# Longer load rows, more output buffers, later stores and single last stores in a fused attention and token-mixing kernel

## The chip, the cores and the metric

The kernel runs on one core of a Trainium2 chip. The metric is the time of one execution on the device in microseconds (us), lower is better. The kernel before takes 130.08 us (median of 3 runs, 130.0 to 131.48). Each run is fast or slow (slow: over 1.5% above the fastest of the same kernel).

The engines are named as in the profile: PE (TensorE) with PEld, its weight loads; DVE (VectorE), ACT (ScalarE), POOL (GpSimd) and SP (SyncE), which issues nearly all DMAs. An eviction is the copy that moves a finished tile from `ps`, which PE writes, to a buffer, for the output to `o_sb` (a median 0.585 us on ACT for a tile of 128x512 in the trace of before).

## The reference

Attention without softmax, in linear form, feeds a token-mixing layer. Cut to what matters:

```python
def _attn_ref(q, k, v):                       # (8, 8, 576, 64) each
    q_p, k_p = phi(q, cos_w, sin_w), phi(k, cos_w, sin_w)   # relu, times cos and sin of position
    kv = np.einsum('bhsf,bhsd->bhfd', k_p, v)
    z = np.sum(k_p, axis=2)
    num = np.einsum('bhsf,bhfd->bhsd', q_p, kv)
    den = np.einsum('bhsf,bhf->bhs', q_p, z)[..., None] + 1e-06
    return num / den

def _moe_ref(x, w_q, w_k, w_out):             # x: (8, 576, 512)
    W_tok = scale * np.einsum('bsd,btd->bst', x @ w_q, x @ w_k)
    mixed = np.einsum('bst,btd->bsd', W_tok, x)
    return np.maximum(mixed, 0.0) @ w_out
```

The inputs q, k and v are 28.3 MB in float32, the output is 9.44 MB.

## The kernel before

A "pair" here is two pairs of heads, that is four of the eight heads of a batch; there are 16, two to a batch. A "block" of the output, numbered 0 to 3, is two batches, 9 tiles of 128 rows, stored in groups of two, two, one, two and two tiles. (The blocks of 256 PE instructions in the experiments are something else.) Every engine's instructions are put in order by a list scheduler in the kernel (`plan_order`) that runs when the kernel is built. Each engine, and SP's queue of DMAs, then goes through its own list in the order of the list. So an instruction whose data isn't there holds up what stands behind it in that list: in the changed kernel two tiles evicted by 109.0 us were stored from 124.0 us on, behind stores of tiles that were evicted later.

```python
PAIRS = ((0, 1), (2, 3), (4,), (5, 6), (7, 8))     # tiles of one store group
CS = ((0, 5), (5, C9))                             # columns: 1280 and 1024 bytes of a row

def load(H, parts=((0, C9),), names=("q", "k", "v"), engs=()):
    for nm in names:
        raw[nm, H] = inp.tile([P, 2, HC], FP32, name="raw")      # 6 buffers
    for lo, hi in parts:
        for nm in names:
            eng = nc.scalar if lo == 0 and nm in engs else nc.sync
            eng.dma_start(raw[nm, H][:, :, lo * D:hi * D],
                          srcs[nm][b][:, h0:h0 + 2, lo * D:hi * D])

def store(bp, g, qs):                              # two DMAs of 64 partitions
    n = len(PAIRS[g])
    for hi in range(2):
        qs[hi].dma_start(..., o_sbs[bp, g][64 * hi:64 * hi + 64, 0:n, :])
...
                elif e == "DMA":
                    key = t            # plan_order: DMAs in the order in which they can start
...
        if kind == "load":
            load(j, parts=CS, names=(b,))
        elif kind == "st":
            last = b == B // 2 - 1 and j >= 2
            store(b, j, (nc.sync, A if last else nc.sync))
```

## Time and profile before

| | before |
|---|---|
| time, median | 130.08 us |
| span of the profiled execution | 129.5 us |
| busy share: PE, DVE, ACT, POOL | 79%, 73%, 61%, 55% |
| last load issued | 95.9 us |
| k multiply of pair 15 begins | 101.48 us |
| last output tile evicted | 123.75 us |

The strip of the profile cuts the span in 40 slices and gives each engine's busy share in tenths. The k multiply (line 392) comes once a pair and serves as a clock of how far the compute has come. The last eviction splits the end into the compute and what the stores need after it. The lines are in the prediction.

The chain of waits that ended last, as shares of the span:

```profile
PE 47%; DMA 19%; DVE 16%; issue 7%; ACT 3%; POOL 2%; SPq 1%; POOLq 0%
```

### The profile page before, as it was taken

To read this page: it belongs to the slowest core of one execution; us is meant where nothing else is said; L and a number is where in the kernel's file an instruction comes from. 1 tells how busy PE (TensorE), PEld (TensorE's weight loads), DVE (VectorE), ACT (ScalarE), POOL (GpSimd) and SP (SyncE) were. 2 spreads that over 40 slices of the span, in tenths; PEclk is the share of its full clock that TensorE was granted. 3 is DMA by queue.
4 is the path that set the end of the run, shared out by engine and by line. 5 is a ranking of instruction groups with operands and counts; after the bars stand their busy time and mean duration, and the time that the engine had idled before them with its cause. 6 is when DMAs were issued, how large, how long until landed. Compare 5 with 4: busy or idle time off the path is not lost.

```text
span 129.5 us, 5391 instructions
## 1 busy us (share of the span) xinstructions
PE 102.7 (79%) x2262; PEld 63.3 (49%) x2286; DVE 95.0 (73%) x156; ACT 79.6 (61%) x155; POOL 71.1 (55%) x113
## 2 busy tenths in 40 slices
PE   5957694757498998979997878998886999998900
PEld 2334353545375644646664645555564655543400
DVE  1067878999789999899989596999899688314000
ACT  6959435083705677687688755864766376656710
POOL 7720557568489999897289287876652710000000
PEclk9999999999756999999999999999999999999995
DMA  3999999999999999999999999999999754667893
GB/s 86 369 359 357 359 309 354 340 337 383 365 356 358 356 358 366 376 378 369 340 356 360 332 308 379 351 347 323 316 318 326 266 133 123 164 166 189 202 210 128
DMA packets 32968, 39.41 MB, mean 304 GB/s; under 512 B 3248, under 2 KB 27824, under 8 KB 32944
## 3 DMA queue, kind: packets, MB, share of 16 engines
q1 hardware_dynamic: 32304, 38.09, 90.9%
q10 hardware_dynamic: 640, 0.98, 2.6%
q8 instruction: 18, 0.29, 0.9%
q14 instruction: 6, 0.05, 0.1%
HBM read 29.62 MB, written 9.44 MB: 302 GB/s over the span
## 4 chain that ended last, share of the span: by engine, by line
PE 47%; DMA 19%; DVE 16%; issue 7%; ACT 3%; POOL 2%; SPq 1%; POOLq 0%
PE ps L563 20%; DMA raw<-in_k_dram 8%; PE ps L493 6%; DMA raw<-in_v_dram 6%; PE ps L453 4%; DVE qpt_buf L420 4%; PE ps L428 4%; DVE x_sb L466 4%; DMA raw<-in_q_dram 4%; DVE kp L392 3%; PE ps L478 3%; PE ps L523 3%; PE ps L539 2%; PE ps L414 2%; POOL rq_buf L379 2%
## 5 line engine op out<-in xcount | busy, mean ns | idle before, releaser
L563 PE MATMUL ps<-wo_sb,mix_sb 128*128 128x512 bf16 x126 | 34.4, 380 | 2.8 <-DVE xT_buf L368 0.9
L379 POOL TENSOR_SCALAR rq_buf<-raw 128x640 bf16<-128x640 f32 (+1 forms) x30 | 26.2, 887 | 16.9 <-DMA raw<-in_q_dram 13.5
L366 ACT COPY o_sb<-ps 128x512 f32<-128x512 f32 x36 | 21.1, 586 | 12.4 <-PE ps L563 11.0
L392 DVE TENSOR_TENSOR kp<-rk,cossin 128x2304 bf16<-128x2304 bf16 (+2 forms) x17 | 23.0, 1352 | 7.8 <-ACT rk L377 6.1
L466 DVE TENSOR_TENSOR x_sb<-ps,rec 128x640 bf16<-128x640 f32 x32 | 26.4, 825 | 1.1
L404 POOL TENSOR_SCALAR v_buf<-raw 128x640 bf16<-128x640 f32 (+1 forms) x26 | 22.5, 879 | 6.2 <-DMA raw<-in_v_dram 3.0
L420 DVE TENSOR_TENSOR qpt_buf<-ps,cst 128x1152 bf16<-128x1152 bf16 x32 | 22.7, 750 | 1.7 <-PE ps L414 1.7
L379 POOL TENSOR_SCALAR rk<-raw 128x640 bf16<-128x640 f32 (+1 forms) x28 | 18.3, 668 | 8.8 <-DMA raw<-in_k_dram 6.2
L563 PEld LDWEIGHTS <-mix_sb 128*128 128x128 bf16 x144 | 12.2, 97 | 14.5 <-issue 2.4
L428 PE MATMUL ps<-v_buf,kp 64*128 64x65 bf16 x576 | 13.1, 193 | 5.7 <-ACT v_buf L402 2.2
L428 PEld LDWEIGHTS <-kp 64*128 64x128 bf16 x576 | 11.1, 95 | 9.5 <-DVE kp L392 5.0
L453 PE MATMUL ps<-kv_sh,qpt_buf 64*128 64x65 bf16 x320 | 14.5, 193 | 1.2 <-issue 1.2
L551 ACT ACTIVATE mix_sb<-ps 128x576 bf16<-128x576 f32 x24 | 14.5, 655 | 1.4 <-PE ps L539 1.3
L453 PEld LDWEIGHTS <-qpt_buf 64*128 64x128 bf16 x640 | 12.9, 96 | 4.9 <-issue 3.9
L453 PE MATMUL ps<-kv_sb,qpt_buf 64*128 64x65 bf16 x320 | 14.5, 194 | 0.1
L368 DVE COPY xT_buf<-ps 128x640 bf16<-128x640 bf16 (+1 forms) x19 | 8.4, 456 | 6.1 <-PE ps L478 3.9
L289 PE MATMUL ps<-warm 128*128 128x512 bf16 x32 | 11.2, 487 | 1.8 <-DVE warm L285 1.5
L414 PE MATMUL ps<-ident,rq_buf 64*128 64x64 bf16 x288 | 8.3, 193 | 3.3 <-POOL rq_buf L379 1.8
L366 ACT CAST wT_buf<-ps 128x576 bf16<-128x576 f32 x8 | 5.1, 637 | 8.2 <-PE ps L493 8.2
L493 PE MATMUL ps<-xT_buf,wqk_sb 128*128 128x288 bf16 x64 | 10.1, 306 | 0.0
L366 ACT CAST kv_sb<-ps 128x260 bf16<-128x260 f32 x15 | 5.6, 375 | 6.9 <-PE ps L428 5.7
L478 PE MATMUL ps<-ident,x_sb 64*128 64x64 bf16 x288 | 7.6, 190 | 2.3 <-DVE x_sb L466 1.5
(51 smaller groups left out, 123.1 us busy)
## 6 DMA issues: line engine op xcount, KB each, us to landing
out_dram<-o_sb SPq DMA_DIRECT2D x30, 256.0 KB, 5.2
raw<-in_q_dram SPq DMA_DIRECT2D x16, 320.0 KB, 6.0
raw<-in_v_dram SPq DMA_DIRECT2D x16, 320.0 KB, 6.2
raw<-in_k_dram SPq DMA_DIRECT2D x15, 320.0 KB, 5.8
raw<-in_q_dram SPq DMA_DIRECT2D x16, 256.0 KB, 5.9
raw<-in_k_dram SPq DMA_DIRECT2D x16, 256.0 KB, 6.0
raw<-in_v_dram SPq DMA_DIRECT2D x16, 256.0 KB, 6.3
wo_f<-in_moe_w_out_dram SPq DMA_DIRECT2D x1, 1024.0 KB, 8.1
```

The source lines that it names most:

```text
L366: nc.scalar.copy(dst, src)
L379: eng.tensor_scalar(dst, src, FMAX, 0.0, op0=ALU.min, op1=ALU.max)
L392: nc.vector.tensor_mul(kp[H][:, 2 * lo:2 * hi], rks[H][:, lo:hi].rearrange("p c i d -> p (c i) d").unsqueeze(2) .to_broadcast([P, 2 * (hi ...
L404: eng.tensor_scalar(dst, src, 1.0, 1.0, op0=ALU.mult, op1=ALU.mult)
L420: nc.vector.tensor_mul(qpt_bufs[H % 2][:, r, :, D:SLOTS * D], bank_h(m)[:, 0:1, 0:HC].to_broadcast([P, 2, HC]), cst)
L428: nc.tensor.matmul(bank(m + r)[:, 0, i * (D + 1):(i + 1) * (D + 1)], kp[H][half_rows(r), 2 * c + i, :, :], v_bufs[H % 3][half_rows(r), c, ...
L453: nc.tensor.matmul(nb[t][:, u, :], qpt_bufs[H % 2][rows, r, w, u * P:(u + 1) * P], mv, start=(u == 0 and w == 0), stop=False)
L466: nc.vector.tensor_tensor(xv[:, h, r], nv[:, :, :, 0:D], rec.to_broadcast([P, 2, SC, D]), op=ALU.mult)
L478: nc.tensor.transpose(bank_h(m + r)[:, 0, k0 * D:(k0 + 1) * D], xs[b][half_rows(r), u, 2 * hp:2 * hp + 2, :], ident[half_rows(r), half_row ...
L493: nc.tensor.matmul(bank(m + nh)[:, 0, 0:hs], wqk_sb[:, dmc, :, :], xT_bufs[b % 2][:, dmc, nh * hs:(nh + 1) * hs], start=(dmc == 0), stop=( ...
L551: nc.scalar.activation(dst, src, AF.Relu, scale=scale_moe)
L563: nc.tensor.matmul(bank(m)[:, 0, :], mixs[bp][:, dmc, rt * P:(rt + 1) * P], wo_sb[:, dmc, :], start=(dmc == 0), stop=(dmc == NDM - 1))
```

## The change

The intent: fetch with longer rows and so less overhead (2304 bytes of a row go as two packets of a median 55 and 46 ns in the trace of before); let loads overtake stores, since the compute waits for loads (POOL for 8.3 us from 80 to 103 us in the trace of before) and no engine that computes waits for a store there; have enough output buffers that nothing waits for a delayed store; and make the last store small. The scheduler's weights were searched anew, and one copy may now go to ACT. The diff, cut to its core:

```diff
-PLAN = dict(mk=1.3, pa=7.848, pc=8.447, pm=8.738, pw=6.677, ... nraw=6, nout=5, ...)
+PLAN = dict(mk=1.3, pa=5.707, pc=6.272, pm=6.005, pw=4.458, ... nraw=6, nout=12, ... ds=11)
...
-        op(("wqc", b), {"DVE": .36}, [("we", b)], 1)
+        op(("wqc", b), {"ACT": .57, "DVE": .36}, [("we", b)], 1)
...
                 elif e == "DMA":
-                    key = t
+                    key = t + (par["ds"] if n[0] == "st" else 0)
...
-    def store(bp, g, qs):
+    def store(bp, g, qs, lo=0, hi=2):          # lo, hi: which tiles of the group
...
         if kind == "load":
-            load(j, parts=CS, names=(b,))
+            load(j, names=(b,))
...
             wout_evac(b, j, m, engs[eng])
+            if b == B // 2 - 1 and j > 4:
+                lo = (j - 5) % 2
+                store(b, (j + 1) // 2, (nc.sync, A), lo, lo + 1)
         elif kind == "st":
-            last = b == B // 2 - 1 and j >= 2
-            store(b, j, (nc.sync, A if last else nc.sync))
+            if b < B // 2 - 1 or j < 3:
+                store(b, j, (nc.sync, nc.sync))
```

More of the change, by code (lines that the diff above doesn't have):

```diff
@@ L22 @@
 EPS_HI = 9.9837780e-07
-PLAN = dict(mk=1.3, pa=7.848, pc=8.447, pm=8.738, pw=6.677, pb=0.821, flex=0.189, poe=11.845,
-            pme=34.049, pmk=1108.864, wo_at=4, nraw=6, nout=5, sw=0, amp=0, seed=99119,
-            sl=0.1, bd=0.2, pact=1)
+PLAN = dict(mk=1.3, pa=5.707, pc=6.272, pm=6.005, pw=4.458, pb=0.728, flex=0.103, poe=2.701,
+            pme=3.798, pmk=160091.523, wo_at=4, nraw=6, nout=12, sw=0, amp=0,
+            seed=32087, sl=0.1, bd=0.2, pact=1, ds=11)
 PAIRS = ((0, 1), (2, 3), (4,), (5, 6), (7, 8))
@@ L500, in wqk_evac, with wq_copy @@
              bank(m, 2)[:, :, 0:hs])
-    def wq_copy(b):
+    def wq_copy(b, eng):
         wq2 = moe.tile([P, S], BF16, name="wq2")
-        nc.vector.tensor_copy(wq2[64:128], wT_bufs[b % 2][0:64, D:SLOTS * D])
+        copy(eng, wq2[64:128], wT_bufs[b % 2][0:64, D:SLOTS * D])
         wqTs[b] = wq2
@@ L571, in wout_evac @@
         copy(eng, o_sbs[bp, g][:, rt - PAIRS[g][0], :], bank(m)[:, 0, :])
-    def store(bp, g, qs):
-        n = len(PAIRS[g])
-        for hi in range(2):
-            qs[hi].dma_start(
-                dataclasses.replace(out, offset=out.offset + out_dest(bp, PAIRS[g][0], hi),
-                                    ap=[[C9 * DM, 64], [2 * DM, n], [1, DM]]),
-                o_sbs[bp, g][64 * hi:64 * hi + 64, 0:n, :])
+    def store(bp, g, qs, lo=0, hi=2):
+        rts = PAIRS[g][lo:hi]
+        for half in range(2):
+            rows = slice(64 * half, 64 * half + 64)
+            qs[half].dma_start(
+                dataclasses.replace(out, offset=out.offset + out_dest(bp, rts[0], half),
+                                    ap=[[C9 * DM, 64], [2 * DM, len(rts)], [1, DM]]),
+                o_sbs[bp, g][rows, lo:lo + len(rts), :])
     A, V, G = nc.scalar, nc.vector, nc.gpsimd
@@ L624, in emit @@
         elif kind == "wqc":
-            wq_copy(b)
+            wq_copy(b, engs[eng])
         elif kind == "wk":
```

## The prediction

The forecast's sum came to 117 + 7.1 = 124.1, and with 0.6 to 124.7. The packet times come from the trace of before.

> **What bounds the kernel now.** I read the strip of 40 slices first, for which resource fills which stretch of the 129.5 us (3.24 us a slice).
>
> ```profile
> span 129.5 us, 5391 instructions
> ...
> PE   5957694757498998979997878998886999998900
> DVE  1067878999789999899989596999899688314000
> ...
> DMA  3999999999999999999999999999999754667893
> GB/s 86 369 359 357 359 309 354 340 337 383 365 356 358 356 358 366 376 378 369 340 356 360 332 308 379 351 347 323 316 318 326 266 133 123 164 166 189 202 210 128
> DMA packets 32968, 39.41 MB, mean 304 GB/s; under 512 B 3248, under 2 KB 27824, under 8 KB 32944
> ```
>
> The DMA row is at 9 from the second slice to the 31st: up to about 100 us the transfers never rest. VectorE is at 9 nearly as long, from 40 to 100 us. Only after that does PE fill its row while DMA and VectorE fall off. So there are two phases: loads until 103 us, and a tail of output matmuls and stores.
>
> Next, the pace of the pairs of heads. The multiplication of k (line 392) runs once a pair on VectorE as soon as k is there, so its starts are a clock. From VectorE's timeline, times in us and durations next:
>
> ```profile
> 13.55 1.35 DVE L392 TENSOR_TENSOR kp<-rk,cossin 128x2304 bf16<-128x2304 bf16 x1
> ...
> 42.97 1.73 DVE L392 TENSOR_TENSOR kp<-rk,cossin 128x2304 bf16<-128x2304 bf16 x1
> ...
> 101.48 1.36 DVE L392 TENSOR_TENSOR kp<-rk,cossin 128x2304 bf16<-128x2304 bf16 x1 [1.17 <-POOL rk L379]
> ```
>
> These are pairs 1, 6 and 15: (42.97 - 13.55)/5 = 5.88 us a pair, then (101.48 - 42.97)/9 = 6.50. A pair loads 3 x 576 KiB = 1.77 MB, 4.97 us at 356 GB/s; pairs 1 to 6 share the queue with 1.31 MB of weights (3.7 us, 0.74 a pair), which makes 5.7. From 47 us stores join: 0.59 MB a pair, and 2.36 MB at 356 GB/s is 6.6 us. Both paces are the DMA's. The windows say the same for the other engines (the columns are the stretch, its length, then busy us of PE, PEld, DVE, ACT, POOL, the clock, DMA share, GB/s):
>
> ```profile
> 50.00:60.00 10.00, 9.03 (x246) 5.94 (x247) 9.48 (x18) 7.78 (x16) 8.64 (x11) 1.00 1.06 374
> ...
> 90.00:100.00 10.00, 8.43 (x230) 5.33 (x232) 9.41 (x17) 6.98 (x16) 5.22 (x9) 1.00 0.99 318
> ...
> 110.00:120.00 10.00, 9.59 (x77) 4.55 (x78) 3.23 (x6) 6.35 (x12) 0.00 (x0) 1.00 0.71 173
> ```
>
> VectorE has half a microsecond in ten left. The DMA is the first bound, and VectorE stands right behind it. GpSimd's waits between 80 and 103 us show who waits for the loads there (us in total, times, longest):
>
> ```profile
> POOL rk L379 <- DMA raw<-in_k_dram: 3.3, 3, 1.7
> POOL rq_buf L379 <- DMA raw<-in_q_dram: 3.2, 3, 1.6
> ...
> POOL v_buf L404 <- DMA raw<-in_v_dram: 1.8, 3, 1.2
> ```
>
> Last, the chain of waits at the end:
>
> ```profile
> 118.66 4.49 PE ps L563 x20
> ...
> 123.17 0.58 ACT o_sb L366
> ```
>
> Five output tiles in 4.49 us, the last eviction done at 123.75, and 5.75 us more for the last stores and the close.
>
> [...] by its packet records a 1024-byte packet takes a median 46 ns, one of 1280 bytes 55 and one of 2048 bytes 84, a slope of about 0.036 ns a byte with 8 to 10 ns on top. [...] Every store here is of 64 partitions; when stores run alone, after 120 us, a 2048-byte packet has a median near 155 ns against 84 before and the rate is 202 to 225 GB/s at a DMA share of 0.85 to 0.9. [...]
>
> **The change part by part.**
> Longer rows. A load has 256 rows, 16 to a DMA engine. Now: 16 x (55 + 46) ns, and two completion packets of 9 ns, 1634 ns; three are 4.90 us, which is the 4.97 found above. After: a 2304-byte packet lies on the line at 91 to 94 ns, so 16 x 92.5 + 9 = 1489 ns. That is 0.145 us a load, and for the 45 loads of pairs 1 to 15, 6.5 us of DMA time. It also halves 90 load issues of some 0.45 us on SyncE, which lie beside transfers and are worth nothing. The price: GpSimd, which still converts in two parts, can't start on the first 5/9 of a tensor, under 0.7 us, felt once or twice.
>
> Deferred stores, twelve buffers. Before the last load is issued (95.9 us) nine store groups have gone: four pairs and a single of the first block, three pairs and a single of the second, 9 x 0.524 MB less two halves = 4.19 MB, 11.8 us at 356 GB/s. The planner's key puts a store behind loads whose buffer comes free up to 11 us later, that is, a shift of nearly two pairs. The groups issued at 82.1, 87.4 and 91.7 should fall behind the last load: a single and two pairs, 1.31 MB, 3.7 us. There are five groups to a block, so twelve buffers hold over two of the four blocks, so no output matmul should wait for one.
>
> So the DMA could bring the last load some 10 us sooner (6.5 + 3.7). I don't credit all of it, because VectorE's work has to be done too. From its groups, work that can't leave it: k multiply 23.0, rotation of q 22.7, normalisation 26.4 + 6.8, sum 78.9 us, 4.93 a pair. The rest of its 95.0, about 16 us or 1.0 a pair, can go to ScalarE (61% busy), and the 4.2 us of the copy at line 504 become movable by this change. If half the 16 moves, VectorE needs 5.4 a pair, at 95% use 5.7; PE's back-to-back runs in the trace (for a pair 0.68 kv, 0.75 numerators, 0.8 transposes; for a batch 2.4 of mixing; for two batches 9 tiles of 0.97) also come to 2.2 + 1.2 + 2.2 = 5.6. Call the pace 5.85: pair 15's multiply at 13.3 + 14 x 5.85 = 95, against 101.5. That is the gain I take, 6.5 us.
>
> From there to the last eviction are 22.3 us now, filled by output matmuls. I leave it at 22, so the last eviction is at 117.
>
> Single stores. The last store moves 128 KB a half rather than 256: at some 220 GB/s 0.6 us less a half, and two queues issue it; 5.75 becomes about 4.3. But there is a danger in the order. The single stores are written right behind their evictions, whereas the groups of tiles 0 to 4 carry the 11 us penalty, also when no load is left to give way to. Tile 8 follows tile 0 by less than 11 us (in the trace of before their evictions start at 123.17 and 112.81), so groups 0 to 2 of the last block, and perhaps the two groups ahead of them, stand on SyncE's queue behind single stores that wait for the last evictions. That would leave 1.3 to 2.4 MB to store at 220 to 260 GB/s after 116 us, 5 to 10 us, an end 9 to 11 us behind the last eviction. I give it an even chance: 0.5 x 4.3 + 0.5 x 10 = 7.1. Sum: 117 + 7.1 = 124.1, and 0.6 for the difference of 130.08 and the span: 124.7.
>
> **Rivals.**
> VectorE takes the DMA's place at once, at 6.1 a pair. For it: it is at 9.5 of 10 already. Against: its row dips between 70 and 80 us (7.46) and after 98, and a third of a batch's evictions may move. Then pair 15 comes at 98.7, the end is 127 to 131, "same".
> The deferred stores pile up at the end, as worked out above: if the compute gains only 5 us, the end is 128 to 129 and the change does nothing.
> Everything goes well: pace 5.6, tail 21, stores 4.3: 13.3 + 78.4 + 21 + 4.3 + 0.6, about 118. For it: GpSimd's 8.3 us of load waits after 80 us go. Against: PE would have to run at its back-to-back rate.
> A load ordered ahead of a ready store waits on its buffer and stops SyncE's queue. It costs only if the output buffers run out, and twelve make that unlikely.
>
> **Range and chances.** 118 and 131 are the ends of the rivals; the middle ones lie at 121 to 129. The limit of 2% is 127.5. It takes one of the two bad rivals nearly in full to miss it, and both together to be slower.
>
> **What would show it.** Right: no 1280-byte packets but pair 0's, a 2304-byte packet at 91 to 94 ns, 375 to 395 GB/s in stretches of loads alone; the last load issued before 90 us; pair 15's multiply at 91 to 99; VectorE at 95% or more from 30 us on with fewer evictions. The danger is real if SyncE's last stores are of tiles 0 to 4 and issue after the last eviction, with the end over 8 us behind it. I am wrong if 2304-byte packets take over 100 ns, if pair 15 isn't before 99, or if PE idles for output buffers.

## The result, and the profile after

The changed kernel takes 138.8 us (138.6 to 139.22, 3 runs). The ratio to the kernel before is 1.064, 95% interval 1.052 to 1.076: slower. A ratio here is the mean time of one kernel's fast runs over that of the other's fast runs of the same rounds, so it isn't quite the ratio of the medians quoted.

First the changed kernel's strip (columns are slices of 3.4 us):

```profile
span 137.0 us, 5308 instructions
...
PE   5968747665899797978898987998989999980000
...
DMA  3999999999999999999999999981074400029994
GB/s 105 372 387 391 362 360 391 390 383 391 392 385 393 387 383 346 387 393 402 398 403 403 395 408 401 385 261 48 7 155 91 145 0 0 5 77 240 248 288 142
```

The loads did what was hoped: mostly 383 to 408 GB/s where mostly 340 to 380 stood before, and they are over at about 89 us. The compute did not follow. PE is still full until 122 us, and while it is, the DMA row goes to 0. Then come 12 us in which no engine computes and the DMA is full again.

The clock of the pairs, from the changed kernel's VectorE timeline (start, duration):

```profile
13.39 1.35 DVE L392 TENSOR_TENSOR kp<-rk,cossin 128x2304 bf16<-128x2304 bf16 x1
...
43.20 1.35 DVE L392 TENSOR_TENSOR kp<-rk,cossin 128x2304 bf16<-128x2304 bf16 x1
...
100.43 1.35 DVE L392 TENSOR_TENSOR kp<-rk,cossin 128x2304 bf16<-128x2304 bf16 x1
```

Pairs 6 to 15 take (100.43 - 43.20)/9 = 6.36 us each, against 6.50 before. Pair 15 is 1.05 us earlier, not 6.5.

The end, from the windows of the changed kernel (stretch, length, busy us of PE, PEld, DVE, ACT, POOL, then clock, DMA share, GB/s), and SP's waits from 82 us on (us in total, times, longest):

```profile
110.00:120.00 10.00, 10.00 (x86) 4.55 (x86) 4.06 (x7) 7.62 (x14) 0.00 (x0) 1.00 0.01 2
...
124.60:137.00 12.40, 0.00 (x0) 0.00 (x0) 0.00 (x0) 0.00 (x0) 0.00 (x0) 0.55 0.82 232
```
```profile
SPq L577 <- ACT o_sb L366: 26.4, 5, 14.4
```

For ten microseconds in which finished tiles lie in their buffers, the DMA moves 2 GB/s, because SP waits up to 14.4 us at a stretch for an eviction. After the last eviction (124.57 us) 12.4 us of stores are left, at 232 GB/s: 2.9 MB.

Split at the last eviction, the two profiled spans compare like this: the compute ends at 124.57 against 123.75 (+0.8), the stores need 12.4 against 5.75 (+6.7). Together that is +7.5 us, 137.0 against 129.5. So there are two questions: why the tail is so long, and why the compute got nothing from loads that were over 12 us sooner (89.5 us against 101.8).

### The profile page after: what moved, and what is told of

The parts are those of the page before. It is cut to its first block, busy times and chain, and to the rows that moved or that the text cites. A ratio compares the mean times of both kernels' runs of the same rounds, so it can differ in the third digit from the quotient of the medians.

```text
span 137.0 us, 5308 instructions
## 1 busy us (share of the span) xinstructions
PE 104.0 (76%) x2279; PEld 62.0 (45%) x2279; DVE 90.7 (66%) x144; ACT 86.9 (63%) x168; POOL 66.3 (48%) x111
## 4 chain that ended last, share of the span: by engine, by line
PE 48%; DVE 15%; DMA 10%; issue 7%; ACT 6%; POOL 2%; ACTq 1%; SPq 1%; DVEq 0%; POOLq 0%
PE ps L563 22%; DMA raw<-in_k_dram 6%; PE ps L493 6%; PE ps L453 5%; PE ps L428 5%; DVE x_sb L466 4%; DMA raw<-in_q_dram 4%; PE ps L478 3%; DVE kp L392 3%; PE ps L523 3%; PE ps L539 2%; DVE qpt_buf L420 2%; DVE mix_sb L553 2%; ACT o_sb L366 2%; PE ps L414 2%
## 5 line engine op out<-in xcount | busy, mean ns | idle before, releaser
L563 PE MATMUL ps<-wo_sb,mix_sb 128*128 128x512 bf16 x144 | 37.1, 388 | 1.6 <-issue 0.9
L366 ACT COPY o_sb<-ps 128x512 f32<-128x512 f32 x35 | 20.6, 590 | 13.2 <-PE ps L563 11.7
L379 POOL TENSOR_SCALAR rk<-raw 128x640 bf16<-128x640 f32 (+1 forms) x28 | 19.3, 708 | 16.2 <-DMA raw<-in_k_dram 9.9
L379 POOL TENSOR_SCALAR rq_buf<-raw 128x640 bf16<-128x640 f32 (+1 forms) x28 | 22.8, 830 | 6.9 <-DMA raw<-in_q_dram 6.2
L404 POOL TENSOR_SCALAR v_buf<-raw 128x640 bf16<-128x640 f32 (+1 forms) x26 | 20.2, 795 | 2.3 <-DMA raw<-in_v_dram 1.6
L366 ACT COPY xT_buf<-ps 128x512 bf16<-128x512 bf16 (+1 forms) x25 | 15.1, 638 | 2.0 <-PE ps L478 1.9
L428 PEld LDWEIGHTS <-kp 64*128 64x128 bf16 x576 | 10.6, 94 | 10.0 <-DVE kp L392 5.7
L551 ACT ACTIVATE mix_sb<-ps 128x576 bf16<-128x576 f32 x20 | 12.5, 661 | 1.9 <-PE ps L539 1.7
L553 DVE TENSOR_SCALAR mix_sb<-ps 128x576 bf16<-128x576 f32 x12 | 8.9, 752 | 6.0 <-PE ps L539 6.0
L289 PE MATMUL ps<-warm 128*128 128x512 bf16 x31 | 9.8, 473 | 1.5 <-DVE warm L285 1.5
```

What stands on the lines that cost most here:

```text
L366: nc.scalar.copy(dst, src)
L379: eng.tensor_scalar(dst, src, FMAX, 0.0, op0=ALU.min, op1=ALU.max)
L404: eng.tensor_scalar(dst, src, 1.0, 1.0, op0=ALU.mult, op1=ALU.mult)
L428: nc.tensor.matmul(bank(m + r)[:, 0, i * (D + 1):(i + 1) * (D + 1)], kp[H][half_rows(r), 2 * c + i, :, :], v_bufs[H % 3][half_rows(r), c, ...
L551: nc.scalar.activation(dst, src, AF.Relu, scale=scale_moe)
L563: nc.tensor.matmul(bank(m)[:, 0, :], mixs[bp][:, dmc, rt * P:(rt + 1) * P], wo_sb[:, dmc, :], start=(dmc == 0), stop=(dmc == NDM - 1))
```

## The experiments

Two kernels are compared by their ratios to the kernel before.

The theories. A: the order on SP's queue makes the long tail. C: transfers set the pace before (the prediction). D: PE or VectorE sets it, whatever the loads do. D gave way to F: the load traffic itself slows PE, by delaying the packets that bring PE's instructions (my reading of the packets that the profile calls "instruction"; they start 3.51 us after a block's start with loads in flight and 1.09 without, see section 3).

### 1. a_tail_order: the late stores in their turn

```diff
+    order = plan_order(NB)
+    # every "st" after the last load moves right behind the last eviction it needs
     for n, eng, m in order:
         emit(n, eng, m)
```

> The changed kernel with the order of every engine kept; only the store groups that are written after the last load are put on SyncE's queue right behind the last eviction that they need, so none stands behind a single store of a later tile. Theory A (the queue order made the long tail): the last eviction stays at 124 to 125 us, the stores end some 5 us behind it, span 129 to 130, about 7 us below the 137.0 of the changed kernel. Rival B (the stores of the last blocks need that time whatever their order[...]): span 135 or more.

Measured: 130.55 us, ratio 1.003 (0.999 to 1.007). Last eviction 123.69, span 128.3: the stores end 4.6 us behind it. The window that moved 2 GB/s now reads:

```profile
110.00:120.00 10.00, 9.84 (x65) 4.44 (x66) 3.68 (x7) 7.41 (x14) 0.00 (x0) 1.00 0.65 160
```

Theory A is shown. With no other instruction moved, some 8 us are gone. The changed kernel's stores on SP stood like this, by the order of its instruction list and the issue times in the trace:

```
SP issue at us   what
105.4            second half of tile 4 of block 2
120.9 122.2 123.4   first halves of the single stores of tiles 5, 6, 7 of block 3
124.0 124.6      tiles 5,6 of block 2      (both evicted by 109.0)
125.4            first half of the single store of tile 8 of block 3
126.1 - 132.9    tiles 7,8 of block 2; tiles 0,1 / 2,3 / 4 of block 3
```

The 11 us of the new key hold also when no load is left to give way to, while a single store is written at its eviction. So 2.36 MB of finished output stood behind stores of tiles that didn't exist yet.

### 2. b_long_rows: the long rows alone

```diff
-            load(j, parts=CS, names=(b,))
+            load(j, names=(b,))
```
(in the kernel before)

> The kernel before with one DMA of 2304-byte rows per load and nothing else changed. Theory C (my prediction: transfers set the pace of the pairs in the kernel before): packets of 91 to 96 ns, some 6 us of DMA time less, pair 15's multiply of k at 95 to 97 us instead of 101.5, time 124 to 126. Rival D (PE, working through its planned order, or VectorE sets the pace, and the DMA is kept busy only because loads run ahead into free buffers): pair 15 not before 100, time 128.5 to 130.

Measured: 134.09 us over four runs, of which the two fast are 131.97 and 133.57; ratio 1.019 (1.011 to 1.028), slower. Pair 15 at 102.35 us, later than before, though a 2304-byte packet has a median of 93 ns as predicted and the last load is issued at 90.1 us instead of 95.9. Theory C falls: faster transfers do not help this kernel and cost it something. Two things in its trace speak to why. Against b_two_pairs (section 3, where block starts are explained) its weight loads are 7.6 us late by the end, and around block starts it loses 8.2 us, more than all of it. And SP's queue stands still more often (waits of this kernel, us in total, times, longest):

```profile
SPq L576 <- ACT o_sb L366: 12.3, 7, 3.7
SPq L576 <- ACT kv_sb L366: 11.2, 4, 4.9
...
SPq L576 <- ACT xT_buf L366: 5.8, 3, 2.2
```

Line 576 is the store. These three lines make 29.3 us of waiting for ACT (which of ACT's instructions is named is inferred). All waits of SP at that line for ACT come to 39.5 us here and to 19.3 us before. Part of it lies in the tail; before that, loads behind such a store wait with it. How much of the loss this makes was not tested.

### 3. b_two_pairs and a_two_pairs: no loads from pair 2 on

```diff
-            raw[nm, H] = inp.tile([P, 2, HC], FP32, name="raw")
+            raw[nm, H] = raw[nm, H % 2] if H > 1 else inp.tile([P, 2, HC], FP32, name="raw")
-        for lo, hi in parts:
+        for lo, hi in parts if H < 2 else ():
```

Their outputs are wrong, which doesn't matter for the times.

> Wrong result on purpose: the kernel before, but only pairs 0 and 1 and the weights are loaded; later pairs read those buffers again. It shows the compute of the old order with no load to wait for. Theory C: the pace of pairs 6 to 15 falls from 6.5 to 5.7 us or less, time below 120. Rival D: the pace stays above 6.1, time 124 to 129.

Measured: 125.41 us, ratio 0.964 (0.958 to 0.970). Pairs 6 to 15 at 6.08 us each (40.40 to 95.13), last eviction at 117.28. C missed both of its numbers. D's time came true, and its pace all but (6.08 against "above 6.1"). Yet the loads do cost 5 us of time, against D's idea that they don't matter.

> Wrong result on purpose: the same two-pair loads in the changed kernel, whose tail still has the stores in their late order. Rival D: pair 15's multiply of k stays within 2 us of 100.4 and the time within 2 us of 138.8, since loads are no longer waited for there. Theory C (the changed kernel still waits for loads somewhere): 3 us or more faster.

Measured: 131.63 us, ratio 1.011, with the bad tail still in it (span 129.9, last eviction 117.75, 12.2 behind it). Pair 15 comes at 93.63, 6.8 us sooner than in the changed kernel, and pairs 6 to 15 take 5.75 us each. The expectation of D misses here, and C's number (3 us or more faster) came true with 7.2. But C's reason did not. Loads cost the changed kernel's compute 6.8 us, although after 45 us hardly anything waits for one to land: POOL's waits for loads are 2.4 us in all from 45 to 90 us. Nor do the instructions themselves get slower: in that stretch both traces have a median of 190 ns for the matmuls of line 428 and of 825 ns for VectorE's line 466.

Where does it go? The PE instructions of the changed kernel and a_two_pairs are the same in the same order, so I compared when each weight load starts in the two traces. The delay doesn't grow evenly. It jumps at every 128th weight load, that is, at every 256th PE instruction, since weight loads and matmuls alternate. Of the 6.8 us, 5.6 come within 17 weight loads around such a place; windows of the same width elsewhere in the 128 gather 0.2 us in the median. The share isn't fixed: in a_tail_order, which has the same compute, it is 3.4 of 6.0 us. The profile has a queue that it calls "instruction"; in this run it moved 18 packets of 16384 bytes:

```profile
q8 instruction: 18, 0.29, 0.9%
```

4558 PE instructions (2279 weight loads, 2279 matmuls) are 17.8 blocks of 256, so about one packet to a block. Such a jump in the changed kernel's timeline of weight loads (start, duration; in brackets the idle time before, "issue" where the engine waited for nothing that the profile shows):

```profile
54.42 0.20 PEld L478 LDWEIGHTS <-x_sb 64*128 64x128 bf16 x9 [1.11 <-issue]
...
60.44 0.17 PEld L478 LDWEIGHTS <-x_sb 64*128 64x128 bf16 x7 [0.57 <-issue]
...
66.64 0.10 PEld L428 LDWEIGHTS <-kp 64*128 64x128 bf16 x2 [0.74 <-issue]
...
73.11 0.37 PEld L428 LDWEIGHTS <-kp 64*128 64x128 bf16 x20 [0.29 <-issue]
...
79.31 0.43 PEld L428 LDWEIGHTS <-kp 64*128 64x128 bf16 x24 [0.79 <-issue]
```

Line 478, 428 or whichever it is: the spot is set by the count, not by the operation. They are 6.0 to 6.5 us apart. Put beside the packet records:

```
blocks of 256 PE instructions that begin between 40 and 86 us, worked out from the traces

kernel           blocks   mean length   packet's start after   next block begins within
                          us            block's start, mean    1.7 us of its landing
after              8        6.02            3.51                  8 of 8
before             8        5.69            2.55                  3 of 8
a_two_pairs        9        5.42            1.09                  1 of 9
b_two_pairs        9        5.57            0.83                  0 of 9
```

In the changed kernel every next block begins 1.4 to 1.7 us after a packet landed. I read this as PE waiting for its own instructions; no record says what a packet holds. The packet itself takes about 1.05 us in both cases; it starts 2.4 us later with loads in flight.

### 4. a_unread_loads: the loads run, but nobody reads them

```diff
+            if H < 2:   # keep pairs 0 and 1
+                raw[nm, H] = consts.tile([P, 2, HC], FP32, name=f"keep_{nm}{H}")
+                into = raw[nm, H]
+            else:       # compute on a kept pair, load into a buffer that is never read
+                raw[nm, H] = raw[nm, H % 2]
+                into = inp.tile([P, 2, HC], FP32, name="raw")
```
(in a_tail_order, with nine output buffers; wrong result)

> Wrong result on purpose: the changed kernel with the mended tail; every load is issued as there (one DMA, rows of 2304 bytes), but from pair 2 on the loads go to buffers that nobody reads, and the compute reads pairs 0 and 1 again. Nothing in the compute can wait for these loads to land. Nine output buffers, so that it fits. Theory F (loads hold PE up through its instruction packets): while loads run, PE's blocks of 256 instructions take 6 us and over, the packet coming 3.5 us after the block's start and the next block 1.4 us after the packet; the time is within 2.5 us of a_tail_order's (ratio to the kernel before 0.98 to 1.0). Rival J (what the loads cost is waiting for them to land and for buffers): blocks as in a_two_pairs, 5.4 us, and a ratio of 0.95 or less.

Measured: 131.93 us, ratio 1.008 (0.999 to 1.017), as slow as a_tail_order, which has 1.003. From 42 us to 92 us the blocks take 5.9 to 6.5 us, the packet starts 3.56 us after a block's start in the mean, and 7 of 8 blocks begin within 1.7 us of its landing. The same window in the changed kernel, in this one, and in a_two_pairs (count of weight loads in the second bracket):

```profile
45.00:90.00 45.00, 39.01 (x919) 23.77 (x918) 36.83 (x57) 32.17 (x68) 35.34 (x49) 1.00 1.04 391
```
```profile
45.00:90.00 45.00, 39.22 (x909) 23.70 (x910) 34.76 (x54) 30.73 (x66) 27.00 (x41) 0.96 1.03 388
```
```profile
45.00:90.00 45.00, 42.11 (x1071) 27.41 (x1079) 40.26 (x62) 36.94 (x81) 30.61 (x44) 1.00 0.45 106
```

918 and 910 weight loads with the traffic, 1079 without. The clock of 0.96 in the middle line is a stretch of 3.4 us at half clock, which can cost 1.7 us at most; the missing 169 weight loads stand for some 7 us (an estimate from 45 us for 1079). No wait of the compute for a load from pair 2 on is left that could explain it, so rival J falls. That the traffic slows the compute is shown. That it does so at the block starts is read from the traces; no run could change the packets themselves.

### 5. Smaller loads: a_tail_half_dma, a_tail_short_rows, b_half_dma

```diff
-                eng.dma_start(raw[nm, H][:, :, lo * D:hi * D], srcs[nm][b][:, h0:h0 + 2, lo * D:hi * D])
+                for i0, i1 in ((0, 1), (1, 2)) if H else ((0, 2),):      # two of the four heads at a time
+                    eng.dma_start(raw[nm, H][:, i0:i1, lo * D:hi * D],
+                                  srcs[nm][b][:, h0 + i0:h0 + i1, lo * D:hi * D])
```

("By head" in the expectations means by pair of heads: two heads to a DMA instead of four.) That the packet waits for whole loads ahead of it, and longer for more rows, is theory F's assumption here. The traces had shown the later start alone: 3.51 us with loads, 1.09 without.

> The changed kernel with the mended tail (as a_tail_order), and each load of 576 KB cut in two DMAs by head: still rows of 2304 bytes, but 8 rows instead of 16 for each DMA engine in one DMA. Theory F (between 45 and 90 us PE is held up once in every 256 of its instructions, because the 16 KB packet that brings its next instructions has to wait for whole loads ahead of it on the same DMA engines, and the wait grows with the rows of one DMA): the packet comes 2 us or less after PE enters a block instead of 3.7, blocks of 256 instructions fall from 6.1 to about 5.5 us, time 126 to 128.5. Rival G (the wait is set by the bytes queued, not by the size of one DMA): the packet still comes 3.5 us after, time 129.5 to 131. Rival H (PE's blocks take that long for another reason): no change either, but blocks don't start at a fixed distance behind the packet.

Measured: 129.6 us over five runs, fast ones 128.32 to 129.84, ratio 0.982 (0.971 to 0.993).

> The changed kernel with the mended tail, but loads in two DMAs by columns, with rows of 1280 and 1024 bytes, as in the kernel before. Theory F: packets of instructions wait some 2 us, as in a_tail_half_dma, and the time is 126.5 to 129, though each load takes 0.15 us of DMA time more. Rival G: as a_tail_order or slower, 130 to 132. If short rows were what kept the kernel before at its pace (my prediction), 132 or more.

(Edit: `load(j, parts=CS, names=(b,))` in a_tail_order.) Measured: 131.64 us, ratio 1.002 (0.992 to 1.011). The packet comes 2.93 us after a block's start, the blocks take 5.73. Less waiting than with whole loads (3.25 in a_tail_order), but the time isn't better: F's number missed. The rows of the kernel before, by themselves, are neither its trouble nor a help here.

> The kernel before with rows of 2304 bytes, each load cut in two DMAs by head. Theory F: the loss of b_long_rows (134.1 median, fast runs 132 to 133.6) goes, time 128.5 to 130.5. Rival G: stays at 132 to 134.

Measured: 130.71 us, fast runs 130.07, 130.16 and 131.26, ratio 0.994 (0.982 to 1.005). What the long rows cost the kernel before in whole loads (1.019) is gone; the packet comes 2.45 us after a block's start against 3.14 in b_long_rows.

These three came from a chip on which the kernel before took 132 us, so the size of the effect was repeated in section 8.

### 6. Who issues the single stores: a_tail_sp_only, a_half_pool_store

```diff
-                store(b, (j + 1) // 2, (nc.sync, A), lo, lo + 1)
+                store(b, (j + 1) // 2, (nc.sync, nc.sync), lo, lo + 1)     # a_tail_sp_only
+                store(b, (j + 1) // 2, (nc.sync, G), lo, lo + 1)           # a_half_pool_store
```

> The changed kernel with the mended tail, both halves of the four single stores issued by SyncE. Theory I (each of ACT's own store issues, 0.5 us, stands between two evictions of the last tiles, which therefore follow at 1.2 us instead of 0.86): the last evictions follow at 0.86 us again, the last one ends 1 us sooner, and the time is 0.5 to 1 us below a_tail_order. Rival: SyncE issues one store after the other at 0.6 us and becomes the end, time equal or longer.

In the changed kernel ACT evicts the last tiles and issues their stores in between, 0.49 to 0.54 us an issue:

```profile
120.34 0.59 ACT L366 COPY o_sb<-ps 128x512 f32<-128x512 f32 x1 [0.28 <-PE ps L563]
120.95 0.54 ACTq L577 DMA_DIRECT2D out_dram<-o_sb  x1
121.59 0.59 ACT L366 COPY o_sb<-ps 128x512 f32<-128x512 f32 x1 [0.67 <-PE ps L563]
122.21 0.50 ACTq L577 DMA_DIRECT2D out_dram<-o_sb  x1
122.83 0.59 ACT L366 COPY o_sb<-ps 128x512 f32<-128x512 f32 x1 [0.65 <-ACT o_sb L366]
```

Tiles follow at 1.25 and 1.24 us. In a_tail_sp_only, from the same view:

```profile
120.52 0.59 ACT L366 COPY o_sb<-ps 128x512 f32<-128x512 f32 x1 [0.28 <-PE ps L563]
121.38 0.59 ACT L366 COPY o_sb<-ps 128x512 f32<-128x512 f32 x1 [0.28 <-PE ps L563]
```

They follow at 0.86 us, so the evictions behave as theory I says, and the last ones no longer wait for ACT. The last one still ends at 123.69, as in a_tail_order, because pair 15 was 1.0 us later in this trace. But the time is 132.51 us, ratio 1.007 (0.996 to 1.018), no better than a_tail_order. SP now issues ten stores after 120 us, one every 0.6, the last at 127.1 us, 3.4 us behind the last eviction. The rival came true: the cost moved from ACT's list to SP's.

> a_tail_half_dma with the second halves of the four single stores issued by GpSimd, which is idle by then, instead of ACT. Theory I: the last evictions follow at 0.86 us instead of 1.2, the last ends 1.1 us sooner, and unlike a_tail_sp_only SyncE has no more to issue than before: ratio some 0.008 below a_tail_half_dma, 0.965 to 0.98. Rival: [...] 0.98 to 0.99.

Measured: 130.07 us, ratio 0.991 (0.982 to 1.000). The last evictions follow at 0.86 us and the last ends at 120.96, but the span is 127.0, 6.0 us behind it. The ratio lies just above the rival's range (0.98 to 0.99), not in theory I's. The rival's reason is cut, since no trace had shown it; in this trace the stores on POOL's queue land a median 3.5 us after their issue, against 3.3 on ACT's queue in a_tail_order.

### 7. Two that led nowhere: a_half_depth5, a_all_ready

a_half_depth5 is a_tail_half_dma with `bufs=5` for the loads and each load moved behind the conversion that frees its buffer.

> a_tail_half_dma with five load buffers instead of six, each load moved in SyncE's order behind the conversion that frees its buffer; all other orders kept. With one load fewer queued, theory F expects the instruction packet some 0.3 to 0.7 us earlier and a time equal to a_tail_half_dma or 1 us less (ratio 0.965 to 0.985). If the compute needs the sixth buffer, GpSimd and ScalarE wait for loads and it is slower (0.99 or more).

Measured: 130.88 us, ratio 0.999 (0.990 to 1.008), the packet 2.86 us after a block's start. POOL waits 7.4 us for loads between 40 and 95 us. Nothing is gained by a shorter queue of loads.

a_all_ready moves every store right behind its eviction, also those before the last load (the edit of a_tail_order without its condition).

> The changed kernel with all stores, not only those after the last load, put right behind the eviction that they wait for: no store is behind a later load any more; twelve buffers, long rows, the plan and the single stores stay. If putting stores behind loads matters to the compute, the last load is issued at 88 to 94 us instead of 82 and the time is 2 us or more above a_tail_order (ratio 1.015 or more). Theory F expects the same time within 1 us (0.995 to 1.01), since loads aren't waited for after 45 us, and no less traffic stands ahead of the instruction packets.

Measured: 133.89 us, but three of four runs were slow, the profiled one too, and no ratio came out. The one fast run is 131.5. The last load is issued at 94.4 us in the (slow) profile. Whether the deferral before the last load is worth anything stays open.

### 8. The sizes again, on one chip with five rounds

> The same kernel as a_tail_order, as the base on this chip: ratio 0.998 to 1.008.

> The same kernel as a_tail_half_dma. If the size of one DMA sets how long PE's instructions wait: 1 to 2 us below tail_again (ratio 0.98 to 0.992), with the packet 2.0 to 2.8 us after the start of a block between 45 and 85 us instead of 3.5. If the first result was chance: within 0.5 us of tail_again.

> The same kernel as a_half_pool_store: the last evictions 0.86 us apart, the last one 1 us sooner than in half_again; if that reaches the end, 0.5 to 1 us below half_again, else equal, because SyncE's queue of stores is then what ends last.

> half_pool_again with the second halves of all the last block's stores on GpSimd, so SyncE has three fewer to issue and nothing of ACT's time is used. If SyncE's issuing ends the kernel, 0.7 to 1.5 us below half_pool_again, ratio 0.97 to 0.985; if the rate of the stores ends it, equal.

half_pool_all is half_pool_again with the second halves of all of block 3's stores on POOL's queue (`(nc.sync, G if b == B // 2 - 1 else nc.sync)`).

| kernel | median us | fast runs | ratio to before | 95% interval | packet after block's start, us |
|---|---|---|---|---|---|
| tail_again | 130.55 | 5 | 0.993 | 0.989 to 0.998 | 3.63 |
| half_again | 129.78 | 5 | 0.987 | 0.982 to 0.991 | 2.80 |
| half_pool_again | 129.78 | 4 | 0.986 | 0.981 to 0.991 | (profile slow) |
| half_pool_all | 130.31 | 3 | 0.984 | 0.978 to 0.990 | (profile slow) |

Halving the DMAs brings the packet 0.8 us sooner, the blocks from 6.08 to 5.68 us, and the time some 0.8 us down (0.0065 x 130). One trace each stands behind the packets: the kernel of tail_again had 3.25 us as a_tail_order, so part of the 0.8 can be chance. The direction agrees with theory F in all three places where loads were cut by pair of heads; cut by columns (a_tail_short_rows) they gained no time. The size is less than expected, and the two intervals overlap. Rival G, that the bytes queued alone set the wait, would give no difference, since the bytes are the same; it is made unlikely, not ruled out. Who issues the last block's stores makes no difference that five rounds can show. The best of these versions are 1.3 to 1.6% faster than the kernel before. No run took the new plan, the twelve buffers or the copy on ACT by itself.

## Why the prediction was wrong

The forecast 124.7 is a sum of 117 for the last eviction, 7.1 for the stores after it and 0.6 for what lies outside the span. The trace has 124.57, 12.4 and 1.8, together 138.8. The three misses are 7.6, 5.3 and 1.2 us.

**"The DMA is the first bound", and from it the gain of 6.5 us at pair 15.** This is the step that failed. The reading was that the DMA row stands at 9, that the paces match the bytes ("Both paces are the DMA's"), and that PE fills its row only after 100 us. But the PE row stands at 7 to 9 from 36 us to the last eviction, but for one slice at 6, and the chain of before holds no transfer after 26.6 us: from 27 to 103 us it is 41.7 us of PE, 20.9 of VectorE and 8.8 of "issue". A match of averages doesn't show who waits for whom; the row can be full because loads run ahead into free buffers (in the changed kernel the DMA share is 1.04 from 45 to 90 us, and POOL's waits for loads are 2.4 us in all). b_long_rows brought the last load 5.8 us sooner and got slower, and a_two_pairs took the loads away and shows the compute at 5.75 us a pair. The pace of 5.85 that I called for is one the engines can do, but only with no load traffic. With it the pace is 6.36. The working went from "more room on the DMA" to "a faster compute" without asking what the traffic does to the compute by itself; none of the four rivals had it. The signs stood in the trace of before: "issue" made 7.3% of its chain, and its pieces at 48.64, 72.18, 77.17 and 99.28 us end where blocks of 256 begin (49.2, 72.6, 77.7, 100.5). They stood in the code as well. `plan_order` of both kernels has a rule for it that the prediction didn't use:

```python
left_in -= PE_COUNT[n[0]]
if left_in < 0:
    left_in += 256
    s = max(s, block)
    block = s + 2.3 + min(3.8, .6 + .8 * max(0.0, free["DMA"] - s))
```

So the planner lets a block begin 2.9 us after the one before at the earliest, and up to 6.1 us after it when loads are queued. That is its writer's assumption, not a measurement; the blocks under load took 6.02 us in the mean.

What cost the kernel before its 6.4 us at pair 15 against b_two_pairs is only partly known: 2.9 us lie around block starts, the rest I could not assign.

**"From there to the last eviction I leave it at 22."** Measured 24.1 (100.43 to 124.57), and 24.1 in a_two_pairs as well, so it isn't the loads. About 1.1 us of the difference is ACT's issuing of single stores between evictions (steps of 1.25, 1.24 and 1.15 us against 0.86), which the prediction counted as a gain ("two queues issue it"). The other 1.0 us is open.

**"I give it an even chance."** The danger was described rightly: the 11 us also without a load, groups 0 to 2 and the two ahead of them behind the single stores, 2.36 MB, "an end 9 to 11 us behind the last eviction". It was 12.4, the sign that the prediction named for this case (last stores of tiles 0 to 4, issued after the last eviction) came true, and a_tail_order shows it as the cause. The chance was the mistake. The order follows from rules in the diff, and the spacing of tiles (10.4 us from tile 0 to tile 8 against a key of 11) was in the text already. An argument that complete deserved nearly all the weight. With 10 in place of 7.1 the forecast would have been 127.6.

**"0.6 for the difference of 130.08 and the span."** The span of 129.5 belongs to the profiled execution, which took 131.6 us, not to the median. Time less span is 2.1 there and 1.8 after.

**Right:** the packets (median 93 to 95 ns against 91 to 94), the rate of loads alone (383 to 408 GB/s against 375 to 395), the last load before 90 us (81.4), no wait for an output buffer, and the change of SP's order. Of these, only the order of the stores set the time. The side remark that a 2048-byte packet takes longer when stores run alone (near 155 ns against 84) is borne out only in part: in the last 12.4 us of the changed kernel the median of a 2048-byte packet was 84 ns, as beside loads, and about a third took over 140 ns.

## What to carry to other kernels

A transfer row that is full is not proof that transfers set the pace (here it stood at 9 up to 100 us, and b_long_rows, with its last load 5.8 us sooner, ran 1.9% longer): run the compute with the loads left out, and again with loads that nobody reads, before paying for faster transfers. If the second is as slow as the kernel with its loads read, the traffic itself is in the way (here 131.93 us in a_unread_loads, ratio 1.008, against 1.003 in a_tail_order); its shape may matter too, though the 0.6% found on one chip has overlapping intervals. The chain of waits is a cheaper first look than either run. And where a rule puts work later "behind" other work, follow it to the end of the list, where there is nothing left to be behind.
